# Moving one more tile's q and k from TensorE transposes to a DMA transpose, with a new order of loads, in a hand-planned attention and MoE kernel

## The chip, the cores and the metric

The kernel runs on one core of a Trainium2 chip. The metric is the device time of one launch in microseconds, the median of several runs; a single profiled execution gives the trace that all durations below come from. Engines: TensorE (PE; its weight loads are listed as PEld), VectorE (DVE), ScalarE (ACT), GpSimd (POOL) and SyncE (SP). DMAs are issued from the queues of POOL, SP and ACT.

## What is computed

For 4 batches, 8 heads, 768 positions and 64 values per head: attention in which a query sees its own last 96 positions and the first 8 positions of the sequence, with a bias that falls with the distance, then a two-layer feed-forward on the rows of all heads together.

```
scores = q @ k.T / sqrt(64)
keep   = (pos_k < 8) | (0 <= pos_q - pos_k < 96)
scores += -slope[head] * (96 if global and not local else |pos_q - pos_k|)
a = softmax(where(keep, scores, -1e9))
x = (a @ v)                       # rows of 3072 tokens, 8 heads side by side: 512 wide
h = x @ w_in                      # 512 -> 2048
out = (h - tanh(h)) @ w_out       # 2048 -> 512
```

Inputs and output are float32; the kernel computes in bf16 with float32 sums.

## The kernel before

**Tiles.** The 3072 tokens are cut into 24 tiles of 128 queries (6 per batch). They run in the order SEQ (line 51): the first tile of each batch (u = 0 to 3), then the other twenty (u = 4 to 23). A tile of the first kind sees only its own 128 keys, a later one its own and those of the tile before it; the 8 global keys and values are copied over the first columns of each tile's own (a_K, a_V).

**Stages of a tile.** Loads of k, q and v (load_bf, line 233, on POOL, which casts to bf16; the first two tiles' k and q come by SP and ACT in float32). Transposes of q and k: head dimension to the partitions. S: scores on TensorE (L315, 8 or 16 matmuls, 64 rows each). E: exp on ScalarE (L324). M: multiplication with the mask on VectorE (L330). AV: values on TensorE (L343, L347). R: division by the sum on VectorE (L355, L356). X: transpose of the attention's output (by TensorE at L370 and a copy at L379 for u < PE_X, by a DMA transpose on SP at L382 after that). m1: first layer (L411), th and g: tanh and subtraction (L423 on ScalarE, L430 on VectorE), m2: second layer (L445), ev: copy out of PSUM (L455), st: store (L460).

**Two ways to transpose q and k.** For tiles u < PE_T (line 57, 6 in this version) a_T (line 267) makes eight TensorE transposes into PSUM (L278; for tiles 2 and 3 sixteen of half the width, L282), and a_Te (line 290) copies them to SBUF on whichever of ScalarE and VectorE the planner finds free (L297). For the others a_DT (line 284) issues one DMA transpose of the 128 x 1024 q and k together on SP's queue (L286), straight from SBUF to SBUF. Loaded q and k lie in a pool of KQ = 3 buffers (kq), which the transposes give back; the transposed ones lie in NK = 8 buffers (qk).

**What sets the order of the work.** Nothing is scheduled when the program runs: plan() (line 658) simulates the kernel while it is built and writes down one fixed list of instructions for each engine. Every step is registered by op() (line 193) with its engine, its assumed duration, what it comes after and which buffers it takes and gives. plan() then again and again takes the candidate that could start earliest (line 792); ties go to pri, attention (0) ahead of m1 and m2 (2). m1 and m2 are queues of pieces, as fillers between the attention steps. On the chip each engine goes through its list in order and waits where an input is late, so a wrong assumption shows as a wait of everything behind it on that engine.

Transfers are modelled by fly_from (line 707) and fly (line 683): a POOL load begins 2 us after its issue, a DMA transpose (keys T and Xe) a given time after its issue, depending on whether POOL loads are in flight; T_LD, T_W, T_DT and so on (line 474) are the times a transfer takes alone, SHARE (line 477) the rates when queues work side by side, FETCHES (line 473) stretches in which no transfer moves, SLACK_DT (line 470) a surcharge on DMA transposes. NUDGE (line 469) can shift the time at which a single step is compared; it is empty here.

**Order of loads.** LOADS (line 482) is written out by hand: t is the next tile's k, q, v (tile 0: v first), i the next of eight pieces of w_in (load_w, L250), o the next of eight pieces of w_out (L252). POOL issues them in that order; a k load must find a free kq buffer.

Of the kernel before, what the change touches and what calls it, by code (L numbers as in the profile page):

```python
# [15 lines left out]
def kernel(  # L16
# [37 lines left out]
    prev_of = {u: pos[t - 1] for u, t in enumerate(SEQ) if t % NQ}  # L54
    head_of = {u: pos[t - t % NQ] for u, t in enumerate(SEQ)}
    PLAIN = 2
    PE_T, PE_X = 6, 9
    HT, LAG, NG = 2, 2.0, 4
    SPLIT = (2, 2, 2)
    TJ = 4  # L60
# [405 lines left out]
    HALVES = 99  # L466
    EB = 2
    INF = 1.0e9
    NUDGE = {}
    SLACK_DT, SLACK_DX = 1.0, 1.0  # L470
    WARM = (1.1, 7.0)
    COLD = 6.3
    FETCHES = [(15.8, 0.9), (23.0, 0.2), (31.0, 0.3)] + [(a, 0.9) for a in (40, 49, 61, 72, 83, 94, 105, 116, 127, 140)]
    T_ROWS, T_LD, T_W, T_ST, T_DT, T_DX = 0.67, 0.89, 1.3, 0.65, 1.05, 0.55
    RING = 5.8
    TAIL = {POOL: 0.45, SP: 0.8, ACT: 0.8}
    SHARE = {
# [1 line left out]
        (True, True, False): (0.36, 0.42, 0), (True, False, True): (0.5, 0, 0.42), (False, True, True): (0, 0.5, 0.42),  # L479
        (True, True, True): (0.3, 0.29, 0.2),  # L480
    }
    LOADS = "tttitiiitiiootooiiotooo"
    first, n_of = [], {"t": 0, "i": 0, "o": 0}
    for c in LOADS + "t" * NU:
        if n_of[c] < (NU if c == "t" else WJ):
# [172 lines left out]
    def plan():  # L658
# [24 lines left out]
        def fly(jobs, t, t_end):  # L683
            fin = {}
            while t < t_end:
                stop = [(a, n) for a, n in FETCHES if t < a + n][:1] or [(INF, 0)]
                if stop[0][0] <= t:
                    t = min(sum(stop[0]), t_end)
                    continue
                heads = [q for q in jobs if jobs[q] and jobs[q][0][1] <= t]  # L690
                later = min([jobs[q][0][1] for q in jobs if jobs[q] and jobs[q][0][1] > t] + [t_end])
                if not heads:
                    t = later
                    continue
                rate = SHARE[tuple(q in heads for q in (POOL, SP, ACT))]
                rate = {q: r for q, r in zip((POOL, SP, ACT), rate)}
                dt = min([later - t] + [jobs[q][0][2] / rate[q] for q in heads])
                dt = min(dt, stop[0][0] - t)
                t += dt
                for q in heads:  # L700
                    jobs[q][0][2] -= dt * rate[q]
                    if jobs[q][0][2] < 1e-6:
                        key = jobs[q].pop(0)[0]
                        fin[key] = t + TAIL[q] + ops[key]["slack"]
            return fin

        def fly_from(q, key, t, end):
            busy = flying[POOL]
            done.update(fly(flying, at_dma[0], t))
            at_dma[0] = max(at_dma[0], t)  # L710
            begin = end + (2.0 if q is POOL else 1.0)
            if key[0] in ("T", "Xe"):
                begin = t + (4.2 if busy else 2.2)
            if q is POOL:
                begin = max(begin, RING)
            flying[q].append([key, begin, ops[key]["dma"], q])
            landed[q].append(key)
            done.update(fly({k: [list(j) for j in v] for k, v in flying.items()}, at_dma[0], INF))
# [3 lines left out]
        def due_at(key):  # L722
            if flies[key] or key not in since:
                since[key] = max(
                    [0.0] + [start[a[1]] if a[0] == "issue" else done[a] for a in ops[key]["after"]]
                )
            return since[key]

        def at_of(x):
            return done[x] if isinstance(x, tuple) else x  # L730
# [18 lines left out]
        while ready or any(queues.values()):  # L749
# [16 lines left out]
            for key, n in cand:  # L766
# [4 lines left out]
                t = free[eng]  # L771
                if o["dma"] and len(landed[eng]) >= 8:
                    t = max(t, done[landed[eng][-8]])
                t = max(t, due_at(key))
                if key[0] == "m1" and t >= due:
                    continue
                if best is not None and round(t + NUDGE.get(key, 0.0), 3) > best[0][0]:
                    continue
                if o["hold"]:
# [3 lines left out]
                    t = max(t, w)  # L783
                for p in set(o["take"]):
                    n_p = o["take"].count(p)
                    if len(avail[p]) < n_p:
                        t = None
                        break
                    t = max(t, sorted(at_of(x) for x in avail[p])[n_p - 1])
                if t is None:  # L790
                    continue
                c = (round(t + NUDGE.get(key, 0.0), 3), o["pri"], n)
                if best is None or c < best[0]:
# [3 lines left out]
            _, key, t, eng = best  # L797
# [7 lines left out]
            if o["at"]:  # L805
                done[key] = o["at"]
            elif o["dma"]:
                fly_from(o["eng"], key, t, end)
            else:
                done[key] = end + LAT[o["eng"]]  # L810
# [95 lines left out]
```

## Time and profile before

| | us |
|---|---|
| median of 5 runs | 212.94 (212.5 to 213.15) |
| profiled execution | 212.59 |
| its span | 210.8 |
| DMA transposes of q and k (L286), 18, issue to landing, least / median / most | 3.4 / 5.6 / 7.8 |
| POOL's waits for a kq buffer (L243 behind qk<-kq), 5 | 13.0 |

TensorE's granted clock was 1.00 in every stretch of 5 us up to 200 us. How to read the rows: an engine's list gives start and length of an instruction, and in brackets how long the engine was idle before it and which instruction's end released it. Matmuls overlap in the pipeline, so the length of one is longer than the distance to the next start; the distance is what it costs. DMA issues are listed with the time from issue to landing; for a single transfer it is asked by a narrow window around its issue. TensorE's busy share includes hidden waits; the list of waits shows those that the profile could attribute.

In the page's row of fortieths of the span (5.3 us each) the DMA engines are busy nine tenths or more from 5 us to 126 us but for one slice of eight tenths, and again from 132 to 142 us; after that half of the time at most.

### The profile page before, as it was taken

How to read it: one execution, taken by the hardware profiler on the slowest of the kernel's cores; microseconds unless marked ns; L12 is line 12 of the kernel's file. 1: busy time of each engine (PE TensorE's matmuls, PEld its weight loads, DVE VectorE, ACT ScalarE, POOL GpSimd, SP SyncE). 2: the span in 40 equal slices, each digit the busy share in tenths (PEclk: the TensorE clock that was granted, in tenths of full speed). 3: DMA queues.
4: the chain of work that ended last, by engine and by line, in shares of the span. 5: the costliest groups of instructions: out<-in, count | busy, mean ns of one | idle time of the engine just before them, and what ended most of it. 6: DMA issues, size and time to landing. Idle time of an engine off the chain costs nothing.

```text
span 210.8 us, 5337 instructions
## 1 busy us (share of the span) xinstructions
PE 204.5 (97%) x2171; PEld 145.2 (69%) x2198; DVE 130.7 (62%) x271; ACT 118.8 (56%) x182; POOL 84.1 (40%) x113
## 2 busy tenths in 40 slices
PE   8899999999999999999999999999999999999993
PEld 2669976876657857656957686668667676666663
DVE  6569875835767878465957595648548494434311
ACT  4767845535575685376648574848466763344420
POOL 8996686626747366466054520920110110111000
PEclk9999999999999999999999999999999999999999
DMA  5999999999999999999989995993510121110112
GB/s 182 180 188 177 190 192 181 188 150 147 246 180 155 180 153 152 151 165 191 122 150 152 125 193 110 115 153 81 123 56 19 60 49 52 53 50 18 37 50 99
DMA packets 104729, 27.49 MB, mean 130 GB/s; under 512 B 94656, under 2 KB 103104, under 8 KB 104704
## 3 DMA queue, kind: packets, MB, share of 16 engines
q0 software_dynamic: 75728, 18.62, 88.1%
q1 hardware_dynamic: 28144, 7.48, 24.1%
q10 hardware_dynamic: 832, 1.05, 1.5%
q8 instruction: 17, 0.28, 0.5%
q14 instruction: 8, 0.07, 0.1%
HBM read 27.26 MB, written 6.29 MB: 159 GB/s over the span
## 4 chain that ended last, share of the span: by engine, by line
PE 94%; DMA 2%; issue 1%; DVE 1%; ACT 0%; DVEq 0%
PE ps L411 41%; PE ps L445 39%; PE ps L315 6%; PE ps L343 3%; PE ps L347 2%; DMA kf<-in_k_dram 2%; PE ps L370 1%; PE ps L278 1%; PE ps L282 1%; PE ps L166 1%; DVE kh L297 0%; DVE kq L256 0%; ACT qk L297 0%; DVE ot L455 0%; DVEq L297 0%
## 5 line engine op out<-in xcount | busy, mean ns | idle before, releaser
L411 PE MATMUL ps<-xT,w_in_bf 128*128 128x256 bf16 (+1 forms) x960 | 96.4, 251 | 0.1
L445 PE MATMUL ps<-w_out_bf,g 128*128 128x512 bf16 (+3 forms) x389 | 89.4, 362 | 1.3
L411 PEld LDWEIGHTS <-w_in_bf 128*128 128x128 bf16 x960 | 77.3, 98 | 16.6
L423 ACT ACTIVATE th<-ps 128x512 f32<-128x512 f32 (+1 forms) x102 | 57.3, 574 | 53.5 <-PE ps L411 51.7
L430 DVE TENSOR_TENSOR g<-ps,th 128x512 bf16<-128x512 f32 (+1 forms) x102 | 64.3, 654 | 35.8 <-ACT th L423 35.4
L445 PEld LDWEIGHTS <-g 128*128 128x128 bf16 x416 | 38.3, 98 | 30.4
L460 POOL DMA_DIRECT2D out_dram<-ot x21 | 11.9, 570 | 88.7 <-ACT ot L455 85.1
L324 ACT ACTIVATE pd<-ps 128x1024 bf16<-128x1024 f32 x24 | 24.6, 1025 | 6.9 <-PE ps L315 6.9
L243 POOL DMA_DIRECT2D kq<-in_k_dram x20 | 17.9, 893 | 16.1 <-DMA qk<-kq 13.0
L324 ACT ACTIVATE po<-ps 128x1024 bf16<-128x1024 f32 x20 | 20.5, 1025 | 4.9 <-PE ps L315 4.9
L237 POOL DMA_DIRECT2D vb<-in_v_dram x24 | 21.7, 904 | 0.2
L455 ACT COPY ot<-ps 128x512 f32<-128x512 f32 x20 | 11.7, 587 | 12.0 <-PE ps L445 12.0
L330 DVE TENSOR_TENSOR po<-po,mk 128x1024 bf16<-128x1024 bf16 x20 | 13.8, 691 | 7.1 <-ACT po L324 7.1
L243 POOL DMA_DIRECT2D kq<-in_q_dram x20 | 17.8, 892 | 0.2
L356 DVE TENSOR_TENSOR x<-ps,rden 128x512 bf16<-128x512 f32 x24 | 16.6, 691 | 0.8
L330 DVE TENSOR_TENSOR pd<-pd,mk 128x1024 bf16<-128x1024 bf16 x20 | 13.8, 689 | 5.3 <-ACT pd L324 5.1
L343 PE MATMUL ps<-vb,pd 128*128 128x65 bf16 x192 | 14.1, 193 | 0.0
L343 PEld LDWEIGHTS <-pd 128*128 128x128 bf16 x192 | 12.5, 98 | 1.0 <-ACT pd L324 0.2
L347 PE MATMUL ps<-vb,po 128*128 128x65 bf16 x160 | 12.4, 193 | 0.0
L315 PEld LDWEIGHTS <-qk 64*128 64x128 bf16 x288 | 8.1, 94 | 5.3 <-issue 5.1
L315 PE MATMUL ps<-qk 64*128 64x128 bf16 x288 | 10.8, 217 | 0.0
L347 PEld LDWEIGHTS <-po 128*128 128x128 bf16 x160 | 10.4, 97 | 0.5
(49 smaller groups left out, 84.9 us busy)
## 6 DMA issues: line engine op xcount, KB each, us to landing
out_dram<-ot POOLq DMA_DIRECT2D x21, 256.0 KB, 3.2
vb<-in_v_dram POOLq DMA_DIRECT2D x24, 128.0 KB, 6.1
kq<-in_k_dram POOLq DMA_DIRECT2D x22, 128.0 KB, 5.3
kq<-in_q_dram POOLq DMA_DIRECT2D x22, 128.0 KB, 5.6
w_in_bf<-in_moe_w_in_dram POOLq DMA_DIRECT2D x8, 256.0 KB, 8.1
w_out_bf<-in_moe_w_out_dram POOLq DMA_DIRECT2D x8, 256.0 KB, 8.8
kf<-in_k_dram SPq DMA_DIRECT2D x2, 256.0 KB, 4.6
qf<-in_q_dram ACTq DMA_DIRECT2D x2, 256.0 KB, 3.8
```

The costliest lines, as they stand in the source:

```text
L237: i = nc.gpsimd.dma_start(out=v_of(u)[:, :, 0:Dh], in_=by_head)
L243: i = nc.gpsimd.dma_start(out=dst.rearrange("p (h d) -> p h d", d=Dh), in_=by_head)
L315: nc.tensor.matmul(s[:, slot(2 * p + hh), :], kT(prev_of[u] if o else u)[r, p, :], qk[u][r, 0, p, :], start=u >= B, stop=True, skip_group_ ...
L324: nc.scalar.activation(pr[u, o].rearrange("q (a h) f -> q a h f", a=2)[:, part], sc[u, o][:, part, :].rearrange("q a (h f) -> q a h f", f= ...
L330: nc.vector.tensor_tensor(out=pr[u, o], in0=pr[u, o], in1=mk[:, :, mask_of(u, o) - 1, :], op=ALU.mult)
L343: nc.tensor.matmul(dst, pr[u, 0][:, slot(h), :], v_of(u)[:, h, :], start=True, stop=last,)
L347: nc.tensor.matmul(dst, pr[u, 1][:, slot(h), :], v_of(prev_of[u])[:, h, :], start=False, stop=True,)
L356: nc.vector.tensor_tensor(out=xs[u].rearrange("q (a h) d -> q a h d", a=2), in0=t[:, :, :, 0:Dh], in1=rden.to_broadcast([P, 2, H // 2, Dh] ...
L411: nc.tensor.matmul(t[:, (f - f0) * n : (f - f0 + 1) * n], w_in_bf[j][:, c, fo : fo + P], xT[b][:, c, o : o + n], start=(c == 0), stop=(c = ...
L423: nc.scalar.activation(h_view(ths[g, f0], g, m), h_view(hs[g, f0], g, m), AF.Tanh, bias=0.0, scale=1.0)
L430: nc.vector.tensor_tensor(out=gs[b][:, f0 : f0 + m, o : o + n], in0=h_view(hs.pop((g, f0)), g, m), in1=h_view(ths.pop((g, f0)), g, m), op= ...
L445: nc.tensor.matmul(os_[u, part][:, 0 : hi - lo], gs[b][:, f, t * P : (t + 1) * P], w_out_bf[f // FJ][:, f % FJ, lo:hi], start=(f == 0), st ...
```

## The change

Five edits, all in numbers that the planner uses, and one of them also decides which code runs. PE_T goes from 6 to 5: tile 5 (the sixth) is transposed by a_DT in place of a_T and a_Te. LOADS is rewritten. The times that plan() assumes for DMA transposes (begin), for loads (T_ROWS, T_LD, T_W) and for the pauses (FETCHES) become slightly shorter. NUDGE gets one entry, for the second quarter of tile 5's m2. No function is changed otherwise.

```
-    PE_T, PE_X = 6, 9
+    PE_T, PE_X = 5, 9
...
-    NUDGE = {}
+    NUDGE = {
+        ('m2', 5, 1): -0.6,
+    }
...
-    FETCHES = [(15.8, 0.9), (23.0, 0.2), (31.0, 0.3)] + [(a, 0.9) for a in (40, 49, 61, 72, 83, 94, 105, 116, 127, 140)]
-    T_ROWS, T_LD, T_W, T_ST, T_DT, T_DX = 0.67, 0.89, 1.3, 0.65, 1.05, 0.55
+    FETCHES = [(15.8, 0.9), (23.0, 0.1), (31.0, 0.1)] + [(a, 0.4) for a in (40, 49, 61, 72, 83, 94, 105, 116, 127, 140)]
+    T_ROWS, T_LD, T_W, T_ST, T_DT, T_DX = 0.66, 0.88, 1.29, 0.65, 1.05, 0.55
...
-    LOADS = "tttitiiitiiootooiiotooo"
+    LOADS = "tttitiitiiiiootoioootoo"
...
             if key[0] in ("T", "Xe"):
-                begin = t + (4.2 if busy else 2.2)
+                begin = t + (3.4 if busy else 2.0)
```

Since plan() starts anew from these numbers, the lists of all engines change behind the first common stretch. On POOL the order of loads is now: tile 4 ahead of w_in 3, w_in 3 to 6 and w_out 0 and 1 ahead of tile 5, then w_out 2, w_in 7, w_out 3 to 5, tile 6, w_out 6 and 7, and the other tiles. On SP there are 19 DMA transposes of q and k, the added one first. The lines behind the NUDGE entry move down by two in the new file (L460 of one is L460 of the other, as all functions named above lie ahead of it).

## Prediction

> **What bounds the kernel now.** I read the page's busy row, then the chain that ended last, then TensorE's own waits.
>
> ```profile
> span 210.8 us, 5337 instructions
> ...
> PE 204.5 (97%) x2171; PEld 145.2 (69%) x2198; DVE 130.7 (62%) x271; ACT 118.8 (56%) x182; POOL 84.1 (40%) x113
> ...
> PE 94%; DMA 2%; issue 1%; DVE 1%; ACT 0%; DVEq 0%
> ```
>
> TensorE carries 94% of the chain; VectorE and ScalarE have over a third of their time free. Busy matmul time alone would not prove saturation, since waits could be hidden in it, so the second view is the list of waits of TensorE over the whole span. It has three rows, and all three lie in the first 8 us:
>
> ```profile
> PE ps L393 <- DVE zero L865: 1.0, 1, 1.0
> PE ps L315 <- ACT qk L297: 0.2, 1, 0.2
> PE ps L278 <- DVE kq L256: 0.2, 1, 0.2
> ```
>
> The same question asked from 14 us to 208 us gives no row at all. A check by addition: I took the built order of before, priced each matmul by its interval in the chain (8 m1 matmuls of 128 columns 0.45 us, of 256 columns 0.87; 4 m2 matmuls 0.86; 16 of S 0.55; 16 of AV 0.48; 4 transposes 0.22) and laid the sum beside the trace. At 17.83 us and again at the first m2 matmul near 27.6 us the trace is 4.7 us later than the sum: no wait between them. At the end (207.6) it is 5.8 us later; the 1.1 us are about 0.1 us after each of the later groups of S (an m1 octet takes 0.98 us behind S and 0.87 elsewhere). So from 14 us on time is the sum of TensorE's work, and only two things can change it: less work, or a wait that is not there now.
>
> **What is removed.** Tile 5's q and k are eight transposes (L278). They are the second and fourth of these rows (the columns are start, length, engine, line):
>
> ```profile
> 28.39 0.39 PE L278 MATMUL ps<-ident,kq 128*128 128x128 bf16 x4
> 28.61 1.03 PE L445 MATMUL ps<-w_out_bf,g 128*128 128x512 bf16 x4
> 29.47 0.39 PE L370 MATMUL ps<-ident,x 128*128 128x128 bf16 x4
> 29.70 0.39 PE L278 MATMUL ps<-ident,kq 128*128 128x128 bf16 x4
> 29.92 1.03 PE L445 MATMUL ps<-w_out_bf,g 128*128 128x512 bf16 x4
> ```
>
> The 0.39 us include the last one's run through the pipeline; what they occupy is the distance to the next start, 28.39 to 28.61 and 29.70 to 29.92: 0.22 us each, **0.45 us** in all. Every other matmul is in both builds in the same number (TensorE's list has 16 rows less, eight weight loads and eight matmuls), and both have 20 groups of S, so no switch is added or saved. The two copies out of PSUM (30.12, 0.76 us for both on VectorE) also go; VectorE idled 0.72 us just before them, so I count nothing.
>
> The Trainium skill has a rule that speaks against this change and a price that speaks for more: "VectorE: DVE Perf Modes", The three transpose paths, gives a bf16 128x128 transpose as 390 ns on TensorE and 1309 ns by DMA, and its rules for authors prefer TensorE where PSUM will do; "TensorE: Matmul & The Clock Gate", Part 4, has about 275 ns inside a kernel. At 275 ns each the eight would give back an estimated 2.2 us. In this trace 219 to 296 ns is how long one lasts, but a new one starts every 56 ns, and the measurement decides.
>
> **What is added, and what hides it.** One DMA transpose of 128x1024 on SP's queue, ahead of the 18 that are there. SP has nothing before it but the two loads at the start; behind it stands the transpose of tile 6, whose inputs land later anyway. Its latency is bounded by the 18 rows of that line: 3.4 least, 5.6 median, 7.8 most. The nearest row is the first of them, issued at 37.51 into a full queue, and the most expensive:
>
> ```profile
> qk<-kq SPq DMA_TRANSPOSE x1, 7.8
> ```
>
> It also takes DMA time from GpSimd's loads. Around that first transpose the k load issued at 34.96 landed 3.0 us after its forerunner where 0.9 is usual, the weights ahead of it were 0.45 late, and the next five loads regained some 0.7: 1.8 us net. Bounds 0 (it fits into gaps) and 2.6 (nothing regained); I take 1.8.
>
> **What is moved.** GpSimd's list: w_in 3 goes behind tile 4's k, q, v; w_in 6 ahead of tile 5, so that tile 5 has 9 weight pieces before it, not 8, and tile 6 has 14, not 13. A piece costs 1.3 us of landing (w_out 0 and 1: issued 16.01 and 17.34, landing 9.4 and 9.3 us later). The planner's constants change no instruction; they change the order that it writes down. TensorE's list is the same through the 16 m1 matmuls of w_in 2 that end at 18.7 us, so the start cannot change. Behind that I count the new list at the rates above, and compare each first use with the landing that the rows of before give:
>
> - w_in 3. Landings of before: w_in 2 at 17.1, w_in 3 18.8, k4 19.7, q4 20.3, v4 22.0 (issue plus landing). As the last of these four it lands at 21.6 to 22.0; its first matmul now stands at 22.2 (in before 19.2). Margin 0.2 to 0.6.
> - Tile 5. q5 landed at 28.4, now 1.3 later, 29.7. Transposed by 35.3 (median) to 37.5 (worst). S of tile 5 stands at 38.5 (in before 33.6). Margin 1.0 at worst.
> - w_out 5. The 14th weight piece: w_out 4 landed at 35.7 as 13th, so 37.0, plus 0 to 2.6, taken 38.8. First use 39.6.
> - Tile 6. q6 landed at 37.4; plus 1.3, plus 0 to 2.6: 38.7 to 41.3, taken 40.5. Transposed 5.6 to 7.8 later: 44.3 to 49.1, taken 48.3. S of tile 6 stands at 48.5. Margin 0.2, and between 4.2 and -0.6. In before it was 2.7 (landed 45.3, S at 48.1). **This is the step at risk.**
> - AV of tile 4 follows its S by 3.1 us of matmuls, not 3.6; in before VectorE was done with the second mask 2.7 us after S. Fits.
> - Tile 9's k load waits for tile 6's buffer (kq has three), so it starts about 3 us later than at 46.31. S of tile 9 stands near 66.5, tile 9 was transposed at 59.8. Fits.
> - S of tiles 12 to 17 stand 1 to 4 us earlier than in before, since the planner believes in quicker transposes. Their margins were 3.9 us (tile 13 landed 86.5, S 90.5) to 9 us. Tight, but positive.
> - Behind 120 us the two lists are nearly the same, 0.45 us apart; the last stores too.
>
> Sum against the profiled execution: 212.59 us (span 210.8 and 1.8 around it) - 0.45 + 0 = 212.14. The median of the runs, 212.94, is 0.35 above that execution; the forecast is 212.94 - 0.45 = **212.5**.
>
> **The rivals.**
>
> 1. The gain is eaten: one of the tight steps (w_in 3, w_out 5, tile 6) is late by 0.2 to 0.6 us. For it: margins of 0.2 us, where loads land up to a microsecond from the row I took. Against: one wait gives all later steps its own length as margin, so only the largest counts, not their sum. -0.45 + 0.4: 212.9.
> 2. Slower, by tile 6. Mechanism: the added transpose takes DMA time from the loads while the queue is full, q6 lands late, its own transpose is at the 7.8 us end, and TensorE's fixed order has S of tile 6 next; everything behind it stands. From 0.9 us of wait on (0.45 for the gain, 0.43 for 0.2%) the kernel is slower. By the rows the end is 49.1 against 48.5, a wait of 0.6; with 0.9 more, as SP's instruction for tile 7's transpose took 2.2 us where 1.3 is usual, it is 1.5. -0.45 + 1.5: 214.0. For it: before's margin of 2.7 us is spent almost whole. Against: it needs the worst end of three terms at once.
> 3. More than the sum: the list of before hides waits that my addition takes for switches after S. Up to 1.1 us are unaccounted; half of that gone gives 212.94 - 0.45 - 0.55 = 211.9.
>
> That the change doesn't do what it says is excluded: the build has 19 DMA transposes at L286 and five tiles through L278 and L282.
>
> **The numbers.** Forecast (no new wait) 0.57, own range 212.2 to 212.8, as the five runs of before spread by 0.3 about their median; rival 1 0.21; rival 2 0.16; rival 3 0.06. The range reaches from 212.0 to 213.4, which leaves out part of rivals 2 and 3. A measurement of this kernel tells about 0.2% from no change, 0.43 us; the forecast of 0.45 lies on that edge, so I give 0.40 of its 0.57 to faster and 0.17 to same. Faster 0.40 + 0.06, same 0.17 + 0.21, slower 0.16.
>
> **What would show it.** Right: TensorE's busy time near 204.1, no row for TensorE among the waits behind 14 us, the chain still at 94%, tile 5's transpose landing before 38.5 and tile 6's before 48.5. Wrong: a wait of TensorE at L315 for qk, or at L411 or L445 for a weight load, between 22 and 50 us; its length less 0.45 is then the change. If the gain is over 0.6 us, the addition above was wrong about the 1.1 us.

## The result, and the profile after

**The changed kernel is slower: 213.27 us (median of 36 runs, 212.78 to 215.84) against 212.48 us (62 runs of the kernel before beside them, 212.18 to 213.59). The ratio is 1.0051, 95% interval 1.0039 to 1.0063.** The forecast was 212.5 us; the time lies inside the range, but on the other side of no change. (A ratio leaves disturbed runs out, none of them here, and is not the quotient of two medians; the means are 213.70 and 212.61 us.)

The times of the changed kernel lie in two groups, 25 runs at 212.8 to 213.7 us and 11 at 214.3 to 215.8 us; of the 62 runs of the kernel before none is above 213.6. The profiled execution of the changed kernel is of the first group: 213.12 us, span 211.3, which is 0.5 us over before. First the page's busy row and the chain that ended last:

```profile
PE 203.8 (96%) x2163; PEld 144.8 (69%) x2190; DVE 128.6 (61%) x262; ACT 121.8 (58%) x189; POOL 84.0 (40%) x113
...
PE 85%; DMA 11%; issue 1%; DVE 1%; POOL 0%; ACT 0%; DVEq 0%; SPq 0%
```

TensorE is busy 0.7 us less, and yet the span is longer: the chain now runs through DMA for 11% of its length (2% before). The waits of TensorE between 14 and 208 us, where before had no row (columns: us in total, times, longest):

```profile
PE ps L315 <- DMA qk<-kq: 1.0, 1, 1.0
PE ps L445 <- issue: 0.2, 1, 0.2
```

The second row is a gap where a matmul's record is missing. The first is real, and TensorE's list shows where it lies:

```profile
36.48 1.89 PE L445 MATMUL ps<-w_out_bf,g 128*128 128x512 bf16 x7
39.41 0.62 PE L315 MATMUL ps<-qk 64*128 64x128 bf16 x16 [1.04 <-DMA qk<-kq]
```

These 16 matmuls are S of tile 5, the tile whose transpose the change moved. TensorE was ready at 38.37 us and stood for 1.04 us, because the DMA transpose issued at 29.53 us took this long to land:

```profile
qk<-kq SPq DMA_TRANSPOSE x1, 9.8
```

It landed at 39.36 us. The last matmul ends at 208.17 us in place of 207.58, 0.59 us later. The wait of 1.04 us, less the 0.45 of work, less a start that is 0.11 us earlier (first m1 matmul at 14.48 us for 14.59) make 0.48 of these; the last 0.1 us was not traced to a step.

Another page row is to be kept in mind, GpSimd's wait for a kq buffer, released by DMA transposes: 20.7 us of waiting where before had 13.0.

```profile
L243 POOL DMA_DIRECT2D kq<-in_k_dram x20 | 17.8, 890 | 25.1 <-DMA qk<-kq 20.7
```

Left to explain: why 9.8 us, where the prediction's worst was 7.8, and the runs at 214.3 us and above, which a wait of 1.0 us cannot make.

### The profile page after: what moved, and what is told of

Read it like the earlier page. It is cut to its first block, busy times and chain, and to the rows that moved or that the text cites. A ratio compares the mean times of both kernels' runs of the same rounds, so it can differ in the third digit from the quotient of the medians.

```text
span 211.3 us, 5320 instructions
## 1 busy us (share of the span) xinstructions
PE 203.8 (96%) x2163; PEld 144.8 (69%) x2190; DVE 128.6 (61%) x262; ACT 121.8 (58%) x189; POOL 84.0 (40%) x113
## 3 DMA queue, kind: packets, MB, share of 16 engines
q1 hardware_dynamic: 29200, 7.74, 25.6%
q10 hardware_dynamic: 832, 1.05, 1.5%
## 4 chain that ended last, share of the span: by engine, by line
PE 85%; DMA 11%; issue 1%; DVE 1%; POOL 0%; ACT 0%; DVEq 0%; SPq 0%
PE ps L445 37%; PE ps L411 34%; PE ps L315 5%; DMA qk<-kq 5%; DMA kq<-in_q_dram 4%; PE ps L343 3%; PE ps L347 2%; DMA kf<-in_k_dram 2%; PE ps L282 1%; PE ps L370 1%; PE ps L278 1%; PE ps L166 1%; POOL kq L243 0%; DVE kh L297 0%; DVE kq L256 0%
## 5 line engine op out<-in xcount | busy, mean ns | idle before, releaser
L430 DVE TENSOR_TENSOR g<-ps,th 128x512 bf16<-128x512 f32 (+1 forms) x102 | 65.0, 655 | 34.8 <-ACT th L423 34.3
L445 PEld LDWEIGHTS <-g 128*128 128x128 bf16 x416 | 38.5, 98 | 30.4
L460 POOL DMA_DIRECT2D out_dram<-ot x21 | 11.9, 569 | 77.7 <-ACT ot L455 74.2
L243 POOL DMA_DIRECT2D kq<-in_k_dram x20 | 17.8, 890 | 25.1 <-DMA qk<-kq 20.7
L362 ACT COPY vb<-vb 8x512 bf16<-8x512 bf16 x11 | 6.8, 618 | 7.8 <-PE ps L347 7.8
```

Of the source, the lines that this page charges most:

```text
L243: i = nc.gpsimd.dma_start(out=dst.rearrange("p (h d) -> p h d", d=Dh), in_=by_head)
L430: nc.vector.tensor_tensor(out=gs[b][:, f0 : f0 + m, o : o + n], in0=h_view(hs.pop((g, f0)), g, m), in1=h_view(ths.pop((g, f0)), g, m), op= ...
L445: nc.tensor.matmul(os_[u, part][:, 0 : hi - lo], gs[b][:, f, t * P : (t + 1) * P], w_out_bf[f // FJ][:, f % FJ, lo:hi], start=(f == 0), st ...
```

## The experiments

All kernels are the changed one with the edit shown, unless the edit is marked as one of before. Since every edit to the planner's numbers makes it write new lists, each run tests its edit together with a new order of everything behind it. "Latency" is issue to landing of a DMA transpose. The letters: W, the loss is the wait of tile 5 and no more; L, the new lists cost as well, in the last runs narrowed to "the shorter assumed latencies leave thin margins"; O, the order of loads costs by itself; S, the transpose is slow because it shares the DMA engines with the loads; F, it is slow because it is the first.

| run | median (runs) | ratio to before, 95% | TensorE's waits in its profile behind 14 us |
|---|---|---|---|
| e1_tile5_on_pe | 213.28 (12) | 1.0032 [1.0009, 1.0055] | none |
| e2_only_pe_t | 215.0 (5) | 1.0105 [1.0079, 1.0132] | 1.1 + 0.9 + 0.5 + 0.4 |
| e3_slack_tile5 | 212.93 (12) | 1.0005 [0.998, 1.0029] | 0.7 (xT), 0.2 (k) |
| e4_old_latencies | 214.23 (7) | 1.0061 [1.0037, 1.0086] | 1.0 + 0.3 (VectorE) |
| p1_loads | 212.9 (12) | 1.0019 [1.0006, 1.0033] | 0.2 (w_in) |
| p2_latencies | 215.21 (7) | 1.0132 [1.0111, 1.0152] | none; second profile 2.5 (S) |
| y_slack_two | 212.98 (12) | 1.0021 [1.0002, 1.004] | 1.2 (S) |
| z_slack_three | 214.25 (6) | 1.0078 [1.0051, 1.0105] | 0.5 + 0.3 (VectorE) |
| x_slack_all | 213.5 (12) | 1.0048 [1.0031, 1.0066] | 0.5 (VectorE), 0.2 |
| v1_slack_where_late | 212.23 (12) | 0.9993 [0.9983, 1.0003] | 0.2 (k) |
| v2_slack_where_late | 213.58 (5) | 1.0048 [1.0035, 1.006] | 0.3 (xT) |

The kernel before had medians of 212.48 to 212.51 us beside these runs. Three of the change's edits stand in this table alone, in before: the transpose costs 1.05% (e2), the order of loads 0.19% (p1), the assumed times 1.32% (p2), and all together 0.51%. They do not add up, as each makes its own lists. The NUDGE entry was not tried alone.

### Is it the wait of tile 5 alone?

**e1_tile5_on_pe: the transpose undone, the rest kept.**

```
-    PE_T, PE_X = 5, 9
+    PE_T, PE_X = 6, 9
```

> The change without its DMA transpose: PE_T back to 6, all other edits kept. Theory W (the whole loss is TensorE's wait at S of tile 5 for that tile's DMA transpose, issued at 29.53 and landed at 39.36, and the rest of the new lists costs nothing): no wait of TensorE at S of tile 5; TensorE's work is 0.45 us more than in the changed kernel, so about the time of before, 212.5 (212.3 to 212.9), TensorE busy near 204.3. Rival L (the new order of loads and the replanned lists cost time themselves): still 213.0 or more, with waits of TensorE at other lines. By its instruction order S of tile 6 stands at 47.0 here, 1.4 us sooner than in the changed kernel, so a wait of up to 0.8 us for tile 6's transpose is possible under both and would have to be taken off before judging.

Measured 213.28 us, and no wait at S of tile 5. W missed: without the added transpose the new lists still cost 0.1% to 0.5%. Its profile has no wait that would say where.

**e2_only_pe_t: the transpose alone, in before.**

```
-    PE_T, PE_X = 6, 9
+    PE_T, PE_X = 5, 9
```

> The kernel before with PE_T = 5 alone: the DMA transpose without the new order of loads and with the old assumed latencies. The planner, cautious, puts S of tile 5 at about 46.2 us, far behind any landing (28.4 plus 10 us). Theory W: no wait for tile 5; TensorE's work 0.45 us less than before. If its later lists hold no wait the time is 212.0; but its S of tiles 5 and 6 come close together at 46 and 48.5, so exp and mask of two tiles follow each other and AV may wait: 212.0 to 213.5. Rival L: same as W here, 212.0, as the old order of loads is kept.

Measured 215.0 us, above the 212.0 to 213.5 of both theories. Tile 5's transpose took 9.7 us here too (28.13 to 37.80), so the order of loads is not what makes it slow. The planner set its S late enough, and the time was lost elsewhere: S waited 1.1 us at 97 us for VectorE (PSUM) and 0.9 us at 65.4 us for tile 9's transpose, which took 10.4 us.

**e3_slack_tile5: the planner told of a later landing.**

```
-... dma=T_DT, slack=SLACK_DT)
+... dma=T_DT, slack=SLACK_DT + (2.5 if u == 5 else 0.0))
```

> The changed kernel with one number: the planner assumes 2.5 us more for tile 5's DMA transpose. S of tile 5 moves 1.7 us back in TensorE's list (from 38.4 to 40.1), other matmuls fill in; S of tile 6 stays at 48.4. Theory W: the wait at S of tile 5 goes; tile 6's transpose landed at 48.69 in the changed kernel and is now the next late one, a wait of 0.2 to 0.6 us: 212.48 - 0.45 + 0.4 = 212.4 (212.1 to 212.8). Rival L: 213.0 or more.

The wait at S of tile 5 is gone, though the transpose took 9.9 us; six of the twelve runs lie at 212.27 to 212.62 us, the other six at 213.25 and up. The profile is of the upper six (213.35 us) and shows a new wait of 0.7 us at 82.34 us, for a DMA transpose of xT of 7.3 us:

```profile
PE ps L411 <- DMA xT<-x: 0.7, 1, 0.7
```

W is half right: without the wait of tile 5 the lower group lies 0.7 us lower (medians 212.46 and 213.16 us), about what the wait had cost, but in this one profiled execution of the upper half another wait takes its place.

**e4_old_latencies: the new order of loads with before's assumed times.**

```
-    FETCHES = [(15.8, 0.9), (23.0, 0.1), (31.0, 0.1)] + [(a, 0.4) for a in (40, 49, 61, 72, 83, 94, 105, 116, 127, 140)]
-    T_ROWS, T_LD, T_W, T_ST, T_DT, T_DX = 0.66, 0.88, 1.29, 0.65, 1.05, 0.55
+    FETCHES = [(15.8, 0.9), (23.0, 0.2), (31.0, 0.3)] + [(a, 0.9) for a in (40, 49, 61, 72, 83, 94, 105, 116, 127, 140)]
+    T_ROWS, T_LD, T_W, T_ST, T_DT, T_DX = 0.67, 0.89, 1.3, 0.65, 1.05, 0.55
...
-                begin = t + (3.4 if busy else 2.0)
+                begin = t + (4.2 if busy else 2.2)
```

> The changed kernel with the old assumed latencies (begin 4.2 and 2.2, old FETCHES, T_ROWS, T_LD, T_W); PE_T = 5, new order of loads and NUDGE kept. S of tile 5 stands at 39.3 in place of 38.4, S of tile 6 at 50.2 in place of 48.4. Theory W: wait at S of tile 5 of about 0.1 us, none at tile 6: 212.48 - 0.45 + 0.1 = 212.1 (211.9 to 212.5). Rival L: 213.0 or more, since the order of loads is the new one.

A miss for W: S of tile 5 begins as its transpose lands (38.99 for 38.95 us), but the new list puts a later S 1.0 us ahead of its PSUM (95.2 us, for VectorE). L's 213.0 us or more came true, but not for its reason: by p1 below, the order of loads is worth far less.

### Why does the transpose take 9.8 us?

**e5_loads_held: GpSimd issues no weights behind w_out 1 until the transpose has landed.** Only the order and the waits differ.

```
-    gate_of = {}
+    gate_of = {("out", 2): ("T", 5)}
...
+        dmas["T", u] = nc.sync.dma_start_transpose(
...
+            load(it, 0.75, lambda it=it: load_w(it), T_W, after=[("T", 5)] if it == ("out", 2) else [])
```

> The changed kernel, but the load of w_out 2, the first one behind tile 5, and with it all later loads, waits until tile 5's DMA transpose has landed. Nothing else is in the DMA engines beside that transpose but v5. The kernel is slower by several us (loads stand still); what is read is the transpose's time from issue to landing. Theory S (the 9.8 us are the shared DMA engines: its packets flow slowly beside the weight loads queued behind tile 5): 3 to 5 us, near the least row of before, 3.4. Rival F (the first DMA transpose of an execution is slow in itself): still 9 to 10 us.

**e6_early_transpose: another transpose of the same size at the start, into a spare tile that nothing reads** (one DMA added).

```
+        nc.sync.dma_start_transpose(
+            out=spare.rearrange("p a b f -> p (a b) f"), in_=slopes.rearrange("p h q -> p (h q)")
+        )
```

> The changed kernel with one more DMA transpose of the same size at the start (of the slopes into an unused tile, some 3 us into the run), so that tile 5's is the second one. Theory S: tile 5's transpose still takes 9 to 10.5 us, TensorE still waits about 1 us at S of tile 5. Rival F: tile 5's takes 6 to 8 us, the wait is gone, and the early one is the slow one.

**e7_tiles_behind: what stands behind the transpose on GpSimd's queue is a tile's k, q and v instead of weights.**

```
-    LOADS = "tttitiitiiiiootoioootoo"
+    LOADS = "tttitiitiiiiootoittooooo"
```

> The changed kernel with another order of loads behind tile 5: w_out 2, w_in 7, then q, k, v of tiles 6 and 7, then the other five w_out pieces. Tile 5's transpose, which moves its data some 4 to 9 us after its issue, then travels beside loads of small packets (256-byte rows of q, k, v) and not of weights (rows of 1 to 2 KB). Theory S in its narrower form (an engine alternates packet by packet, so big neighbours slow the transpose): 7 to 8.3 us, as tile 6's in before (7.8, beside k, q, v loads). Rival F, or sharing without regard to packet size: 9 to 10 us. The time itself will be worse, since w_out comes late.

Latencies of tile 5's transpose: alone **3.16 us** (e5), with another transpose before it 9.47 us (e6), beside k, q and v 8.02 us (e7), beside weights 9.8 us. The rows of e5 and e7:

```profile
qk<-kq SPq DMA_TRANSPOSE x1, 3.2
qk<-kq SPq DMA_TRANSPOSE x1, 8.0
```

F falls with e6 and e5; S holds. In e6 the wait at S of tile 5 was only 0.4 us, where 1 was expected, as its first m1 matmul came 1.5 us later. (As kernels the three took 219.61, 214.51 and 219.16 us, one run each: in e5 and e7 what was held back is late elsewhere, in e6 the added DMA makes the first loads late.) What is shared can be read from the packets of the two queues in a window of one microsecond (columns: packets, MB, share of 16 engines; q0 is GpSimd's loads, q1 SP's transposes). In after from 34 to 35 us, beside weights:

```profile
q0 software_dynamic: 158, 0.16, 92.7%
q1 hardware_dynamic: 155, 0.04, 29.7%
```

In before from 43 to 44 us, the transpose of tile 6 beside k, q and v:

```profile
q1 hardware_dynamic: 414, 0.11, 79.9%
q0 software_dynamic: 415, 0.05, 79.9%
```

In e5 from 31 to 32 us, the transpose with no load beside it (the first row is the busy share in 40 slices of the window):

```profile
DMA  0000000000000000002258799999999899999999
...
q1 hardware_dynamic: 414, 0.11, 52.9%
```

Where both queues have work, they move the same **number of packets**: 158 and 155, 415 and 414. A transposed tile is 1056 packets, 1024 of them of 256 bytes (the page counts 29200 packets of this queue in after and 28144 in before, one tile apart). Beside k, q and v, whose packets are of 128 bytes (0.05 MB in 415), some 400 of the transpose's pass in a microsecond: tile 6's in before passed from 41.5 to 44.7 us, in 3.2 us. Beside weights of 1 KB a packet (0.16 MB in 158) only 155 pass: tile 5's in after passed from 33.7 to 38.5 us, in 4.8 us, and sped up behind 35 us, as the weights ran out. That is 1.7 of the 2.0 us between 7.8 and 9.8.

The Trainium skill states such a rule: "DMA: Bandwidth & Descriptors", Queues, rings and completion order, says that each DMA engine goes round its queues and changes from one to the next at packet boundaries. The equal counts agree with it, though whether a row of the trace is what the page calls a packet, some 9 to 17 descriptors, no run here shows. The rule would have been a reason to ask ahead of time whether a price taken beside 128-byte packets holds beside 1 KB ones.

The rest of the latency lies mostly ahead of the first packet, and there the two do not differ: 4.2 us in after (29.5 to 33.7) and 4.0 us in before (37.5 to 41.5), with GpSimd's loads queued. In e5 the queue's first packets show 1.3 us behind the issue (30.18 to 31.45 us). What makes the difference of nearly 3 us was not tried apart.

**e8_after_again: the changed kernel itself, unedited.**

> The changed kernel once more, for a second profile: its timed runs spread from 212.8 to 215.8. Theory W: the wait at S of tile 5 is there again, 0.8 to 1.5 us, as tile 5's transpose lands 9.5 to 10.5 us after its issue. If this execution is a long one, a second wait shows; by the slack experiment the likeliest is m1 of tiles 8 and 9 waiting for the DMA transpose of tile 9's attention output, near 82 us.

212.99 us, latency 9.9 us, wait 0.8 us at S of tile 5 and nothing else. In all twelve profiles in which tile 5 goes by DMA with weights behind it, the latency is 9.46 to 10.11 us: the late landing is no accident of one run.

### Why are some runs 1.5 us slower still?

**p1_loads and p2_latencies: the two other halves of the change, each alone, in before.** The first:

```
-    LOADS = "tttitiiitiiootooiiotooo"
+    LOADS = "tttitiitiiiiootoioootoo"
```

> Before with the new order of loads alone (six tiles by TensorE, the old assumed latencies). The study's second run (tile 5 back on TensorE, all else changed) was 0.3% to 0.5% slower without any wait for tile 5, so something besides the transpose costs. Theory O: the order of loads itself costs, 213.1 to 213.8 here. Theory L: it is the shorter latencies assumed by the planner, which put users closer to the landing of what they use; with the old latencies the planner knows of the new order and stands clear: 212.5 (212.2 to 212.9), no wait of TensorE behind 14 us.

The second is the diff of e4 the other way round, in before:

```
-                begin = t + (4.2 if busy else 2.2)
+                begin = t + (3.4 if busy else 2.0)
...
```

> Before with the new assumed latencies alone (six tiles by TensorE, the old order of loads). TensorE's amount of work is before's. Theory L: the users of the DMA transposes (the groups of S, the m1 matmuls behind a transposed xT) stand 1 to 4 us closer to their landing and some wait: 213.0 to 213.8, with waits at S or at m1 for a DMA. Theory O: 212.5 (212.2 to 212.9), no new wait.

Order of loads: 212.9 us, ratio 1.0019, with a wait of 0.2 us for w_in at 22.2 us, where the prediction had a margin of 0.2 to 0.6. Shorter assumed latencies: **215.21 us, ratio 1.0132**, more than the whole change. O is worth at most a third of a percent; L has the direction right, and its range for p2 (213.0 to 213.8) was too low. But the profiled execution of p2 was one of the two of its runs below 213 (212.76 us) and shows no wait; the other five lie at 215.05 to 216.13. Hence two more profiles of p2, and one more of the changed kernel.

**p2_second_look, p2_third_look, after_second_look** (no edits to p2 and to after):

> The kernel with the shorter assumed latencies alone once more, for its profile: its timed runs lie in two groups, 212.5 to 212.8 and 215.0 to 216.1, and the profiled one was of the first. Theory L (thin margins): a profile of the second group, 215.0 or more, has waits of TensorE for a DMA transpose at groups of S (near 69 or 72 us, where the first profile had a margin of about zero) whose lengths add up to the 2.5 us between the groups. Rival: no new wait, and the matmuls themselves last longer in the second group.

> As the run before it: of seven timed runs five lay near 215.2, so one of two more profiles should. Theory L: 215.0 or more, with waits for DMA transposes of 2 to 2.6 us in all. If both profiles fall at 212.8 or less, the second group stays unexplained.

> The changed kernel itself once more, for its profile: 25 of its 36 timed runs lie at 212.8 to 213.7, 11 at 214.3 to 215.8. Both profiles so far are of the first group and show 0.8 and 1.0 us at S of tile 5. Theory L: a profile of 214.3 or more has a second wait, at S of tile 9 or 10 or at an m1 octet behind a DMA transpose of xT, of 1.2 to 2 us. Below 213.7: the wait at tile 5 alone, 0.8 to 1.2 us.

The third profile of p2 was of neither kind (213.66 us: 0.5 us at the start, and no further wait). The second was at 216.91 us, and its waits of TensorE behind 14 us are

```profile
PE ps L315 <- DMA qk<-kq: 2.5, 2, 2.3
```

The longer one is S of tile 9, released at 64.99 us; in the first profile the same S began at 62.38 us without a wait, 3.2 us behind its transpose's landing (59.15). Before's list has it at 65.01 us, 5.2 us behind the landing (59.76). The new profile of after was at 215.17 us, of the slower group, and its waits behind 14 us are

```profile
PE ps L411 <- DMA xT<-x: 1.8, 1, 1.8
PE ps L315 <- DMA qk<-kq: 0.7, 1, 0.7
PE ps L411 <- DMA w_in_bf<-in_moe_w_in_dram: 0.6, 1, 0.6
```

Besides tile 5's wait it has two that the first profile has not: the m1 matmuls of a new xT at 84.23 us, and a weight load at 18.1 us. The instruction that waited longest:

```profile
84.23 2.45 PE L411 MATMUL ps<-xT,w_in_bf 128*128 128x256 bf16 x21 [1.75 <-DMA xT<-x]
```

Following the transfer back through the issue and landing times of the first and of this slower profile of after (the q load of tile 9 was issued at 50.76 and 50.94 us, so at nearly the same time, and took 6.6 and 8.8 us; from there on to the next tile's transpose on SP each step starts when the one above it has landed):

| step | first profile | slower profile |
|---|---|---|
| q of tile 9 lands | 57.35 | 59.69 |
| its transpose (issue, landing) | 57.50, 64.52 | 59.84, 66.85 |
| k load into the freed buffer issued | 65.05 | 67.38 |
| q load behind it (issue, landing) | 65.93, 70.54 | 68.26, 75.13 |
| transpose of that tile issued on SP | 70.69 | 75.27 |
| xT's transpose behind it on SP (issue, landing) | 75.06, 80.17 | 76.61, 84.19 |
| first m1 matmul on this xT | 82.19 | 84.23 |

This is a loop: three kq buffers, a load that needs one, a transpose that gives it back, and SP's queue in which everything stands in order. Lateness is handed on in it (2.3 us at the first landing, 2.3 at the reload, 4.6 at the next transpose). At the transpose of xT most of it goes: in the first profile that one waited for its own input (VectorE wrote x until 75.03 us), in the slower one for its place on SP, 1.55 us later. The other 2.5 of the 4.0 us by which it lands later are a longer flight, 7.6 for 5.1 us, close behind the other transpose; that the two share the queue's packets is likely, not shown. The steps that a list puts close behind a landing pay for it. The shorter assumed latencies put them closer, as S of tile 9 in p2 shows. That the eleven runs of the upper group all have such waits rests on this one profile.

### Can the margins be given back?

**y_slack_two** (slack for tile 5, and behind xT), **z_slack_three** (also tile 6), **x_slack_all** (behind every transpose):

```
-    SLACK_DT, SLACK_DX = 1.0, 1.0
+    SLACK_DT, SLACK_DX = 1.0, 2.5
...
-... slack=SLACK_DT)
+... slack=SLACK_DT + (2.5 if u == 5 else 0.0))
```

This is y. In z tile 6 gets 1.0 besides; x has 3.0 and 2.0 in the first line and no second edit.

> After, with 2.5 us more between tile 5's transpose and its S in the planner, and 2.5 in place of 1.0 us behind the transposes of xT. Both waits seen so far (S of tile 5; m1 of tile 9 behind its xT at 82 us) have their cover back. Theory L: nothing is left but the 0.45 us less work: 212.2 to 212.7, ratio 0.998 to 1.000. Theory O: still 213.0 or more. If it is 212.8 and up with a wait at S of tile 6 (margin 0.05 us in the run with slack for tile 5 alone), the third thin margin is the next to pay.

> As the run with slack for tile 5 and xT, and 1.0 us more for tile 6: the planner moves S of tile 6 from 48.4 to about 50.1 us, and other groups of S by up to 1.8 us. Theory L: 212.1 to 212.6, better than or equal to the run beside it, and no wait of TensorE behind 14 us. Theory O: 213.0 or more. A third outcome, that the moved groups of S wait for PSUM instead (a wait for VectorE or ScalarE at L315), would give 213 and up with that row in the list of waits.

> After, with 2.0 us more of assumed delay behind every DMA transpose of q and k, and 1.0 more behind those of xT; the amount of work is after's. Theory L: with margins of 1 us and more everywhere the second group of runs goes, and the 0.45 us shows: 212.1 to 212.6, narrow. Against it stands the run with slack for three places, where moved groups of S waited for PSUM: then 213.0 and up, with waits at L315 or L445 for VectorE.

All three missed L's range. In y the profile (213.75 us) has no wait at tile 5 or xT and 1.2 us at S of tile 10, whose transpose took 9.4 us (61.95 to 71.35): the next thin margin. The profiles of x and z have no wait for a transpose at all, and waits of the third kind named in z's expectation: the group of S near 94 us comes 6.6 (x) and 7.2 us (z) behind the one before it, where after has 8.3, and waits for VectorE, which has yet to free its PSUM. In x:

```profile
94.88 0.60 PE L315 MATMUL ps<-qk 64*128 64x128 bf16 x15 [0.49 <-DVE g L430]
```

These two profiles are the fastest of their runs (213.04 and 213.38 us); what makes the medians 0.5 and 0.9 us longer was not profiled.

**v1_slack_where_late, v2_slack_where_late: slack only where a transpose was seen late, and the S groups kept apart.**

```
-    SLACK_DT, SLACK_DX = 1.0, 1.0
+    SLACK_DT, SLACK_DX = 1.0, 2.2
...
-... slack=SLACK_DT)
+... slack=SLACK_DT + {5: 2.5, 6: 0.5, 9: 0.7, 10: 1.2}.get(u, 0.0))
```

This is v1; v2 has 2.5 for the 2.2.

> After, with slack put just where waits were seen: 2.5 us for tile 5, 0.5 for tile 6, 0.7 and 1.2 for tiles 9 and 10, and 2.2 in place of 1.0 behind xT. S of tiles 6, 9 and 10 move 0.9 us later, S of tile 13 0.9 us, so that (unlike in the two runs with slack in more places) no group of S comes close behind the group before it. Theory L: the narrow lower group of the run with slack for tile 5 is the whole distribution: 212.1 to 212.6, ratio below 1.000, no wait of TensorE behind 14 us but 0.1 to 0.2. If an upper group from 213 on remains, feedback from transpose to reload moves the lateness to whatever is next, and slack in places does not remove it.

> As the run before it, with 2.5 behind xT and S of tile 13 at 1.7 us later than in after. Theory L: 212.1 to 212.6 again. The two differ little, so a large difference between them would say that the planner's order elsewhere, and not the margins, sets the time.

v1 is the version that the waits pointed to: **212.23 us (212.0 to 213.17, eleven of twelve at 212.53 or less), ratio 0.9993, interval 0.9983 to 1.0003.** The page's rows for its profiled execution:

```profile
span 210.3 us, 5347 instructions
...
PE 205.7 (98%) x2190; PEld 144.8 (69%) x2190; DVE 127.6 (61%) x264; ACT 120.7 (57%) x187; POOL 84.1 (40%) x113
...
PE 94%; DMA 4%; POOL 1%; DVE 0%; issue 0%; POOLq 0%
```

The chain is back at 94% TensorE. Its S of tile 5 begins without a wait, though that transpose still took 9.55 us (29.46 to 39.01):

```profile
37.66 2.54 PE L445 MATMUL ps<-w_out_bf,g 128*128 128x512 bf16 x11
40.12 0.62 PE L315 MATMUL ps<-qk 64*128 64x128 bf16 x16
```

The last matmul ends at 207.11 us, 0.47 before the 207.58 of before, and the execution takes 212.06 us, 0.53 less. (Its first m1 matmul starts 0.41 us earlier than before's, but a wait for k at 18.5 us takes that back; the 0.47 us come behind it. Busy time does not compare here: this trace has all 2190 matmuls, those of before and after miss 27.) The interval of the timed ratio still touches 1, so faster than before is seen in the traces and in the medians (0.25 us), not proved by the timing. It is faster than the changed kernel by 1.0 us in the medians, in another set of runs.

v2 differs little and is at 213.58 us. Its profile (213.74 us) has 0.5 us at the start, 0.3 us behind xT, and about 1 us at the end, where the last store took 2.64 us to land and v1's 1.56 us; its last matmul ends at 207.73 us. From the first m1 to the last matmul the two take the same time, 192.93 us in v1 and 193.02 in v2, so the margins hold in both; but the expectation that the times agree failed, and why the start and the last store are late in v2 was not found.

## Why the prediction was wrong, point by point

1. **The removed work, 0.45 us: right.** The last matmul of v1, in which the waits for transposes are gone, ends 0.47 us earlier than before's, though the medians differ by 0.25 only. Nothing shows the larger gain of rival 3.
2. **The price of the added transpose: the step that failed.** The prediction bounded the latency at 3.4 to 7.8 us and took 7.8 as "the nearest row ... and the most expensive", with S at 38.5 and a "margin 1.0 at worst". S was where it said (38.37 us) and the issue too (29.53 for 29.7), but the latency was 9.83 us. The sum had "+ 0" for new waits on this ground. The nearest row in time was not the nearest in kind: in before the packets of the first transpose pass beside k, q and v, the last weight lands at 42.59 us and the other 17 are issued behind 46 us, so none of the 18 rows was measured beside more than a last few weights. This one runs beside 1 KB weight packets, packet for packet, and its own packets took 4.8 us in place of 3.2. The margin of 1.0 was a wait of 1.0.
3. **The loads: close, and harmless in this execution.** w_in 3 landed at 20.93 us (taken 21.6 to 22.0), w_out 5 at 37.64 (38.8), q6 at 40.6 (40.5). The term of 1.8 us for DMA time taken from the loads was too high for the weights.
4. **Tile 6, "the step at risk": right as a margin of about zero.** It landed at 48.69 us (taken 48.3). The wait at tile 5 covered it in after (S at 49.47); in e3, where that wait was gone, its S began at 48.83 us, 0.05 us behind the landing. The prediction's sentence that one wait gives all later steps its length as margin held, in that stretch.
5. **"S of tiles 12 to 17 stand 1 to 4 us earlier ... Tight, but positive": the second step that failed.** It read each margin from one execution, and said of the planner's constants that they "change no instruction" but only the order, without a price for that order. Alone they cost 1.3% (p2). Transposes of the same step landed 7.6 us and 5.1 us after their issue in two executions of one kernel, so a margin of 2.0 us (xT at 82 us) was no margin. It also stopped at S, and never priced m1 behind xT.
6. **Rival 2 (slower, 214.0): the mechanism and the sign were right, the tile and the size were not.** The wait came at tile 5, 1.0 us long, not at tile 6 with 1.5. It had 0.16 of the chance because it was thought to need three worst ends at once; one was enough, beyond the end assumed.
7. **Rival 1** (a wait of 0.2 to 0.6 us at w_in 3): seen in p1 (0.2 us at 22.2 us) and not in after's first profile.
8. **The base was high, and the range held by luck.** The forecast was reckoned from 212.94 us, the median of five runs; over 62 runs the kernel before has 212.48. From there the same sum gives 212.0, so that the measured time misses it by 1.2 us and not by 0.8.

What stays open: what makes a load land 2 us later in one execution than in the next, so that the loop starts late; and the 0.8 us by which e1's median exceeds before's. Its profile (213.16 us) has 0.25 us of them at the last matmul and 0.3 behind it, and none as a wait behind 14 us; so the wait at tile 5 is shown to cost what it lasts, 0.55 us net of the work, but not to be the only thing by which the new lists lose. No profile of e1's upper runs was taken, and none of p1's beyond the first.

## What to carry to other kernels

A DMA's latency is priced by what runs beside it in its own stage, down to the size of the packets of the other queue, and not by the worst row of other stages. Where a fixed order is planned from assumed latencies, making them shorter is an edit as large as any: its price is the spread of the landings over several executions, and one profile that shows no wait says nothing of the other group of a kernel whose times lie in two. Slack belongs to the steps seen late; slack everywhere moved the waits of the profiled executions to PSUM. That v1 gained and v2, nearly the same, did not, says that such a gain has to be measured each time.

## What was not expected of the hardware

- Two DMA queues share by packets, not by bytes: 158 against 155 packets in a microsecond is 0.16 MB against 0.04 MB. Tile 6's transpose in e7, issued at 35.09 us while tile 5's was under way and with weights beside it, took 12.8 us.
- A wait can cost more than its length. In the second profile of p2, TensorE stood 2.32 us ahead of 64.99 us, and afterwards its granted clock fell. The rows are stretches of 2 us, the clock stands after POOL's busy time:

```profile
64.00:66.00 2.00, 1.01 (x21) 0.86 (x22) 0.17 (x1) 0.57 (x1) 0.51 (x1) 1.00 2.57 153
66.00:68.00 2.00, 2.00 (x16) 1.65 (x14) 0.88 (x2) 1.86 (x3) 2.00 (x3) 0.62 1.40 265
68.00:70.00 2.00, 2.00 (x12) 1.44 (x11) 1.91 (x4) 0.60 (x1) 1.30 (x3) 0.53 2.16 162
70.00:72.00 2.00, 1.95 (x29) 1.61 (x28) 1.17 (x4) 1.46 (x3) 2.00 (x3) 1.00 2.09 209
```

The clock was 0.62 and 0.53 of full for these 4 us (half from 66.47 to 69.88 us), and the 16 m1 matmuls at 66.81 us lasted 3.42 us where 16 of before last 1.91. 212.76 us of the first profile and 2.5 of waits make the 215.2 near which most of p2's runs lie; the other 1.6 us to this one's 216.91 fit the low clock, which by an estimate from these 3.41 us at half takes 1.7.

Two other profiles show the same fall, each time to half and for 3.41 us: e7 at 47.90 us, as a wait of 3.06 us ended, and e5 at 40.27 us, where no idle stretch was over 1.14 us but three of 1.0 to 1.1 us and one of 0.5 lay between 34.84 and 39.88 us. Single waits of 1.0 to 1.75 us (after, e4, y, the slower profile of after) left the clock at 1.00. The Trainium skill, "TensorE: Matmul & The Clock Gate", Part 1, gives an idle window of about 3.4 us for this step down. No idle stretch here was that long, and in e5 several short ones were followed by it; the measurement decides.
